# Pairing the odd token tiles of an attention + FFN kernel, with gate sums in other places, two single units and reordered last stores

## The chip, the cores and the metric

The kernel runs on one core of one Trainium2 chip. The metric is the device time of one execution in microseconds. Before the change the median of three runs is 400.83 us (400.82 to 401.29). The profile is one further execution; its run took 400.93 us, its span is 399.2 us.

## What is computed

```python
# q, k, v: (8 batches, 12 heads, 448 tokens, 64)
scores = (1 / sqrt(64)) * q @ k.T - log(448)
attn   = sigmoid(scores)
x      = (attn @ v)            # heads side by side: (3584 tokens, 768)
gate   = maximum(x @ w_gate, 0)        # (768, 1536)
val    = x @ w_val                     # (768, 1536)
out    = (gate * val) @ w_out          # (1536, 768), float32
```

The matmuls run in fp16 with fp32 sums.

## The kernel before

**Layout.** A batch has 448 tokens; two batches make a group of 896 tokens, four groups in all. The hidden activations of a group lie in hT: 12 units of 128 hidden features (on the partitions) by 896 tokens. 896 tokens are seven token tiles of 128; the seventh, tile 6, is the odd one.

**Attention.** A score unit (qk_unit, line 292) is one of 21 per batch: three groups of four heads by seven key chunks. It makes 4 matmuls into two PSUM banks, and ScalarE puts a sigmoid over each bank (line 187). After seven units of a head group, the PV matmuls (line 250) read the probabilities, and VectorE evicts two banks to xT (line 184).

**FFN in batches 0 and 1.** The ordinary form (gv, line 304): six matmuls for the gate, six for the value, a relu, and a multiply into hT (line 327).

**FFN in groups 1 to 3.** A fast 2x2 block product with seven block products in place of eight (Strassen-Winograd), in two places. In gv_pair (line 498) the blocks are halves of the 768 features, gate against value, and one batch of the group against the other; one item takes two units of 128 hidden features at once and holds six PSUM banks: b, c and a, each for two units. In down_pair (line 423) the blocks are two token tiles, halves of the hidden features, and halves of the output; it holds three banks b, c and a. In both the bank b is filled, copied out, and then accumulated on again; so is c. The order of products and copies in gv_pair is:

```python
product(b, 0, B11);  copy(0, b, first_copy)   # first_copy: VectorE, in the tail ScalarE
product(c, 3, T1);   copy(2, c)               # ScalarE
product(b, 4, T2, False);  copy(1, b)         # ScalarE
beside()                                      # next item's sums, then the slot's jobs
product(a, 1, B21);  plus(0, a)               # VectorE
product(b, 5, T3, False);  plus(2, b)
product(c, 6, B22, False); plus(1, c)
product(b, 2, T4, False)                      # then the gating: even batch, odd batch
```

The sums of blocks are made on VectorE: token_sums (line 406, four of 128x768), unit_sums (473, three of 128x768), batch_sums (492, over xT), weight_sums (395, over w_out, 128x2304), and gate_sums (469), which overwrite half of w_val once the ordinary form no longer needs it.

**Odd tiles.** Three pairs take tiles 0 to 5 of a group. Tile 6 goes through down (line 341): 12 matmuls of 512 columns and 12 of 256.

**Order of the work.** The order on every engine is the order of the program text; nothing reorders it. From batch 2 on, a batch is cut into slots: some score units (with the PV matmuls of a head group after the second unit in slots 0, 2 and 4), then one item from a hand-written queue named work (push_group, line 653; next_work, line 667). "Slot 4.1" below is slot 1 of batch 4. The items are w (a gate/value pair of units), y0 to y2 (a pair of token tiles) and t (the odd tile). prepare (line 659) makes the sums of the item that comes next. jobs are copies and DMA transposes for the next batch, loads, and batch sums; they stand inside the item, after its first copy (y) or after its third product (w). PSUM banks come from a ring of eight; later() chooses which banks are taken again last.

Of the kernel before, what the change touches and what calls it, by code (L numbers as in the profile page):

```python
# [17 lines left out]
def kernel(  # L18
# [244 lines left out]
    class FirstSlot:  # L263
# [6 lines left out]
        def unit(self, u):  # L270
            qn = self.qn
            cs = range(2 * u, min(2 * u + 2, NCH))
            ps = pairp.tile([P, 2, 512], FP32, tag="pair", name="qk_ps")
            for j, c in enumerate(cs):
                qk(
                    qkT_tiles[(0, self.g)], c, self.c0, self.c1,
                    lambda hh: ps[:, hh, j * qn : (j + 1) * qn],
                )
            i = (self.number * 4 + u) % 12
            PT = early.tile([P, 2, 512], FP16, tag=f"PT{i}", name="PT")  # L280
            n = qn * len(cs)
            sigmoid(PT[:, :, 0:n], ps[:, :, 0:n])
            for j in range(len(cs)):
                self.pieces.append(PT[:, :, j * qn : (j + 1) * qn])

# [17 lines left out]

    def gv(b, q0, qn, f, act_relu):
        ps = []
        for nm, wt in (("g_ps", wg), ("v_ps", wv)):
            ps.append(bank(nm))
            for dc in range(NDC):
                nc.tensor.matmul(  # L309
                    ps[-1][:, 0:qn],  # L310
                    wt[:, dc, f * P : (f + 1) * P],
                    xT_tiles[b][:, dc, q0 : q0 + qn],
                    start=(dc == 0),
                    stop=(dc == NDC - 1),
                )
        gate_sb = gsbp.tile([P, S], FP32, tag="gsb", name="gate_sb")
        if act_relu:
            nc.scalar.activation(gate_sb[:, 0:qn], ps[0][:, 0:qn], AF.Relu)  # L318
        else:
            nc.vector.tensor_scalar(  # L320
                out=gate_sb[:, 0:qn], in0=ps[0][:, 0:qn], scalar1=0.0, scalar2=None, op0=AOP.max
            )
        g = b // 2
        if g not in hT_tiles:
            hT_tiles[g] = hTp.tile([P, NFC, 2 * S], FP16, tag="hT", name="hT")
        o = (b % 2) * S + q0
        nc.vector.tensor_tensor(  # L327
            out=hT_tiles[g][:, f, o : o + qn],
            in0=gate_sb[:, 0:qn],
            in1=ps[1][:, 0:qn],  # L330
            op=AOP.mult,
        )
# [8 lines left out]
    def down(g, t):  # L341
        ysb = ysbp.tile([P, DM], FP32, tag="ysb", name="ysb")
        for nm, m0, m1 in (("ya", 0, 512), ("yb", 512, DM)):
            ps = bank(nm)
            for f in range(NFC):
                nc.tensor.matmul(  # L346
                    ps[:, 0 : m1 - m0],
                    hT_tiles[g][:, f, t * P : (t + 1) * P],
                    wo[:, f, m0:m1],
                    start=(f == 0),  # L350
                    stop=(f == NFC - 1),
                )
            nc.vector.tensor_scalar(
                out=ysb[:, m0:m1], in0=ps[:, 0 : m1 - m0], scalar1=OUT_SCALE, scalar2=None, op0=AOP.mult
            )
        store(g, t, ysb, 0, DM, (nc.sync, nc.sync))

# [7 lines left out]
    late = {}  # L365
    sums = {}

    def open_late():
        first_sbuf.close()
        pool = ctx.enter_context(tc.tile_pool(name="late", bufs=1))  # L370
        late["T"] = pool.tile([P, 4, HF, HM], FP16, tag="T", name="T")
        late["X"] = pool.tile([P, 3, HD, S], FP16, tag="X", name="X")
        late["sums"] = ctx.enter_context(tc.tile_pool(name="sums", bufs=2))
# [20 lines left out]

    def weight_sums(i):
        T = [late["T"][:, j] for j in range(4)]
        B11, B21 = wo[:, 0:HF, 0:HM], wo[:, HF:NFC, 0:HM]
        B12, B22 = wo[:, 0:HF, HM:DM], wo[:, HF:NFC, HM:DM]
        sub(T[i], *((B12, B11), (B22, T[0]), (B22, B12), (B21, T[1]))[i])

    def token_blocks(g, p):
        h = hT_tiles[g]
        t1, t2 = (slice(t * P, (t + 1) * P) for t in (2 * p, 2 * p + 1))
        return h[:, 0:HF, t1], h[:, HF:NFC, t1], h[:, 0:HF, t2], h[:, HF:NFC, t2]
# [18 lines left out]
    def down_pair(g, p, beside, then, last, first_copy):  # L423
        A11, A12, S3, A22 = token_blocks(g, p)
        S1, S2, S4 = sums.pop(("y", g, p))
        T1, T2, T3, T4 = (late["T"][:, i] for i in range(4))
        B11, B21, B22 = wo[:, 0:HF, 0:HM], wo[:, HF:NFC, 0:HM], wo[:, HF:NFC, HM:DM]
# [23 lines left out]
        plus(y2[:, hi], b)  # L451
        product(c, S4, B22, False)
        plus(y1[:, hi], c)
        if last:
            store(g, 2 * p, y1, 0, DM, (nc.sync, nc.scalar))
        else:
            store(g, 2 * p, y1, 0, DM, (nc.sync, nc.sync))
# [3 lines left out]
        if last:  # L461
            store(g, 2 * p + 1, y2, HM, DM, (nc.sync, nc.sync))
            store(g, 2 * p + 1, y2, 0, HM, (nc.sync, nc.scalar))
        else:
            store(g, 2 * p + 1, y2, 0, DM, (nc.sync, nc.sync))
# [7 lines left out]
    def unit_sums(g, f):  # L473
        S1, S2, S4 = sums_tile(2 * P)
        fs = slice(f * P, (f + 2) * P)
        A11, A12 = wg[:, 0:HD, fs], wg[:, HD:NDC, fs]
        S3, A22 = wv[:, 0:HD, fs], wv[:, HD:NDC, fs]
        sub(S2, A22, S3)
        nc.vector.tensor_tensor(out=S1, in0=S2, in1=A11, op=AOP.add)
        sub(S4, A12, S2)  # L480
        sums[("w", g, f)] = S1, S2, S4
# [10 lines left out]
    def batch_sums(g, ks):  # L492
        T1, T2, T4, _, B21, B12, B22 = batch_blocks(g, ks)
        sub(B12, B22, B12)
        sub(T2, B22, T1)
        sub(T4, B21, T2)

    def gv_pair(g, f, beside, first_copy):
# [3 lines left out]
        b, c, a = ([bank(nm) for _ in range(2)] for nm in ("u", "g2", "g1"))  # L502
        later((6, 7, 4, 5, 2, 3))
        gs = [[gsbp.tile([P, S], FP32, tag="gsb", name="gsb") for _ in range(3)] for _ in range(2)]
        if g not in hT_tiles:
            hT_tiles[g] = hTp.tile([P, NFC, 2 * S], FP16, tag="hT", name="hT")
        h = hT_tiles[g]
        sets = []
        for u in range(2):
            us, fs = slice(u * P, (u + 1) * P), slice((f + u) * P, (f + u + 1) * P)  # L510
            S1, S2, S4 = (t[:, :, us] for t in sums[("w", g, f)])
            sets.append((
                wg[:, 0:HD, fs], wg[:, HD:NDC, fs], wv[:, HD:NDC, fs],
                S1, S2, wv[:, 0:HD, fs], S4,
            ))
        del sums[("w", g, f)]

        def product(ps, i, W, first=True):
            for u in range(2):
                products([(ps[u], S, HD, sets[u][i], W, first)])  # L520

        def copy(i, ps, by=nc.scalar.copy):
            for u in range(2):
                by(gs[u][i][:], ps[u][:, 0:S])  # L524

        def plus(i, ps):
            for u in range(2):
# [3 lines left out]

        def gated(u, o, gate_sb, val):
            nc.vector.scalar_tensor_tensor(
                out=h[:, f + u, o : o + S], in0=gate_sb, scalar=0.0, in1=val, op0=AOP.max, op1=AOP.mult
            )
# [15 lines left out]
        for u in range(2):  # L551
            gated(u, 0, gs[u][0][:], b[u][:, 0:S])
        for u in range(2):
            gated(u, S, gs[u][1][:], gs[u][2][:])
# [97 lines left out]

    def push_group(g):
        tail = [("t", g, 6)] + [("y", g, p) for p in range(3)]
        if g == 0:
            tail.insert(0, tail.pop(1))
        work.extend([("w", g, f) for f in range(0, NFC, 2) if g > 0] + tail)
# [9 lines left out]
    def next_work(jobs=(), alone=False):  # L667
        kind, g, i = work.popleft()

        def beside():  # L670
            for job in jobs:
                job()

        if kind == "y":
            down_pair(g, i, beside, prepare, not work, scaled_act if alone else scaled)
        elif kind == "w":
            gv_pair(g, i, lambda: (prepare(), beside()), nc.scalar.copy if alone else nc.vector.tensor_copy)
        else:
            beside()
            prepare()  # L680
            down(g, i)

    ffn_mix(1, [(1, lambda: both(1, 0))])
    for b in range(1, B):
# [16 lines left out]
        elif b == 2:  # L701
            mix = (2, 2, 1, 1, 1, 2)
            hooks = {
                2: [(0, prepare)],
                4: [(1, lambda: weight_sums(0)), (0, lambda: weight_sums(1))],
# [3 lines left out]
        elif b == 3:  # L709
            mix = (1, 1, 1, 0, 0)  # L710
        else:
            mix = (0,) * count
        for m in range(count):
            jobs = []
            for i, (g, c) in enumerate(order[cuts[m] : cuts[m + 1]]):
                if m in pv_at and i == pv_at[m][1]:
                    if m == 0:
# [3 lines left out]
                        elif b % 2 == 0:  # L721
                            push_group(b // 2 - 1)
# [5 lines left out]
            if b == 2 and m == count - 1:  # L728
                jobs.append(lambda: (dma_transposes(3, 0), dma_transposes(3, 1)))
            elif b == 3 and m == count - 1:  # L730
# [12 lines left out]
            if b % 2 and b > 2:  # L743
                if m == count - 1:
                    jobs.append(lambda: (batch_sums_t1(b // 2), batch_sums(b // 2, (0, 1))))
            elif b > 3 and m == 0:
                jobs.append(lambda: batch_sums(b // 2 - 1, (1, HD)))
            if b == 2 and m == count - 1:
                ffn_mix(mix[m], hooks[m])
                next_work(jobs)  # L750
# [6 lines left out]
            if b == 3 and m == 3:  # L757
                for f in range(0, NFC, 2):
                    gate_sums(f, f + 2)
    pv_finish(B - 1)  # L760
    push_group(B // 2 - 1)
    next_work([lambda: batch_sums(B // 2 - 1, (1, HD))])
# [32 lines left out]
```

## Time and profile before

| | |
|---|---|
| runs | 400.82, 400.83, 401.29 us |
| span of the profile | 399.2 us, granted clock 0.999 |
| busy | PE 388.9, DVE 279.9, ACT 223.0, POOL 49.4 us |
| chain that ended last | PE 73%, DMA 14%, issue 6% |
| matmul groups L385 (block products) | from 93.5 us to the end |
| last matmul ends, last copy ends | 393.8, 394.65 us |

PE is TensorE's matmuls, PEld its weight loads, DVE VectorE, ACT ScalarE, POOL GpSimd, SP the queue that issues stores and transposes. In a timeline a line gives start and length in us, engine, line of the code, operation, what is written and read, how many instructions were merged, and in brackets how long the engine was idle before and what released it. In the list of waits the numbers are the total in us, how often, and the longest.

The items stand thus in the slots:

| where | before | after |
|---|---|---|
| 2.5, 3.3, 3.4 | y0, t, y1 | y0, y1, y2 |
| 4.0 to 4.4 | y2, w, w, w, w | w, w, w, w, w |
| 5.0 to 5.4 | w, w, t, y0, y1 | w, y3, y0, y1, y2 |
| 6.0 to 6.4 | y2, w, w, w, w | w, w, w, w, w |
| 7.0 to 7.4 | w, w, t, y0, y1 | single, single, y0, y1, y2 |
| after the last batch | y2, six w, t, y0, y1, y2 | six w, y3, y0, y1, y2 |

### The profile page before, as it was taken

The numbers are of one execution on the slowest core, as the hardware profiler recorded it, in microseconds if no ns is written. First come the engines' busy times: TensorE is split into PE (matmuls) and PEld (weight loads), VectorE is DVE, ScalarE is ACT, GpSimd is POOL, SyncE is SP. The second block draws the span as 40 slices with busy tenths as digits, with TensorE's granted clock in tenths as the row PEclk, the third lists the DMA queues.
The fourth block names the chain that finished last, engine by engine and source line by source line (L and its number), as shares of the span: only waits on it lengthen the run. The fifth ranks groups of instructions, "written<-read, shape, count | busy, mean of one in ns | idle before, by whom it ended". The sixth has DMA issues, their size and how long they took to land.

```text
span 399.2 us, 8737 instructions
## 1 busy us (share of the span) xinstructions
PE 388.9 (97%) x3488; PEld 217.9 (55%) x3488; DVE 279.9 (70%) x539; ACT 223.0 (56%) x475; POOL 49.4 (12%) x73
## 2 busy tenths in 40 slices
PE   8999999999998999999999999999999999999994
PEld 3678786545455554554555555455455555555562
DVE  2454344367358889999758889999766779887661
ACT  5946778783885565655665455565566234533131
POOL 8643301600030300003000300000000000000000
PEclk9999999999999999999999999999999999999999
DMA  9999994999897894224945695223012320000144
GB/s 149 199 199 204 205 141 94 177 203 187 178 161 152 165 204 76 46 48 51 178 85 133 130 218 89 48 24 61 12 40 80 80 79 2 0 2 0 39 115 124
DMA packets 68793, 43.69 MB, mean 109 GB/s; under 512 B 35856, under 2 KB 65296, under 8 KB 68752
## 3 DMA queue, kind: packets, MB, share of 16 engines
q0 software_dynamic: 30736, 23.33, 39.1%
q1 hardware_dynamic: 37584, 19.24, 23.0%
q8 instruction: 27, 0.44, 0.5%
q10 hardware_dynamic: 432, 0.56, 0.4%
q14 instruction: 14, 0.11, 0.1%
HBM read 47.19 MB, written 11.01 MB: 146 GB/s over the span
## 4 chain that ended last, share of the span: by engine, by line
PE 73%; DMA 14%; issue 6%; POOL 3%; DVE 2%; ACT 1%; ACTq 0%; POOLq 0%; DVEq 0%
PE u L385 32%; PE g L385 15%; PE y L385 9%; DMA v<-in_v_dram 6%; PE qk_ps L232 5%; PE pv_ps L250 5%; DMA wo<-in_moe_w_out_dram 4%; DMA k<-in_k_dram 4%; PE ya L346 3%; PE v_ps L309 1%; PE yb L346 1%; PE g_ps L309 1%; POOL q L110 1%; POOL k L110 1%; DVE wv L376 1%
## 5 line engine op out<-in xcount | busy, mean ns | idle before, releaser
L187 ACT ACTIVATE PT<-qk_ps 128x448 f16<-128x448 f32 (+3 forms) x318 | 150.6, 594 | 71.2 <-PE qk_ps L232 71.1
L385 PEld LDWEIGHTS <-S 128*128 128x128 f16 x540 | 52.8, 98 | 44.4 <-issue 0.8
L528 DVE TENSOR_TENSOR gsb<-g,gsb 128x448 f32<-128x448 f32 x72 | 43.0, 625 | 14.5 <-PE g L385 13.8
L232 PE MATMUL qk_ps<-qkT 64*64 64x448 f16 (+2 forms) x756 | 50.0, 336 | 0.9 <-DVE qkT L206 0.5
L421 ACT ACTIVATE ysb<-u 128x384 f32<-128x384 f32 x27 | 13.4, 498 | 56.3 <-PE u L385 56.3
L327 DVE TENSOR_TENSOR hT<-gate_sb,v_ps 128x256 f16<-128x256 f32 (+2 forms) x36 | 16.2, 465 | 33.5 <-ACT gate_sb L318 22.4
L385 PEld LDWEIGHTS <-hT 128*128 128x128 f16 x288 | 27.7, 98 | 21.0 <-issue 3.2
L524 ACT COPY gsb<-u 128x448 f32<-128x448 f32 x48 | 25.8, 566 | 23.9 <-PE u L385 22.9
L250 PE MATMUL pv_ps<-PT,v 64*64 64x448 f16 (+2 forms) x756 | 37.4, 329 | 0.4 <-issue 0.4
L184 DVE TENSOR_SCALAR xT<-pv_ps 128x448 f16<-128x448 f32 (+2 forms) x53 | 27.9, 567 | 13.4 <-PE pv_ps L250 12.1
L232 PEld LDWEIGHTS <-qkT 64*64 64x64 f16 x756 | 20.3, 105 | 24.9 <-issue 16.3
L309 PE MATMUL v_ps<-xT,wv 128*128 128x256 f16 (+2 forms) x216 | 33.3, 291 | 0.4 <-DVE hT L327 0.2
L309 PE MATMUL g_ps<-xT,wg 128*128 128x256 f16 (+2 forms) x216 | 33.5, 292 | 0.1
L385 PEld LDWEIGHTS <-wv 128*128 128x128 f16 x216 | 21.1, 98 | 19.8
L385 PEld LDWEIGHTS <-wg 128*128 128x128 f16 x216 | 20.3, 98 | 20.6 <-issue 3.0
L250 PEld LDWEIGHTS <-v 64*64 64x64 f16 x756 | 21.8, 107 | 11.8 <-issue 1.4
L385 PE MATMUL u<-T,hT 128*128 128x384 f16 x144 | 27.3, 326 | 0.0
L437 DVE SCALAR_TENSOR_TENSOR ysb<-y,ysb 128x384 f32<-128x384 f32 x24 | 13.4, 557 | 18.8 <-PE y L385 11.3
L110 POOL DMA_DIRECT2D k<-in_k_dram x14 | 10.9, 779 | 112.3 <-DVE rel L215 105.8
L309 PEld LDWEIGHTS <-wg 128*128 128x128 f16 x216 | 18.5, 98 | 11.5 <-issue 5.0
L309 PEld LDWEIGHTS <-wv 128*128 128x128 f16 x216 | 20.1, 98 | 8.2 <-DMA wv<-in_moe_w_val_dram 0.5
L385 PE MATMUL u<-xT,wg 128*128 128x448 f16 x108 | 23.5, 353 | 0.1
(67 smaller groups left out, 531.3 us busy)
## 6 DMA issues: line engine op xcount, KB each, us to landing
out_dram<-ysb SPq DMA_DIRECT2D x53, 192.0 KB, 2.9
k<-in_k_dram POOLq DMA_DIRECT2D x5, 672.0 KB, 11.8
q<-in_q_dram POOLq DMA_DIRECT2D x5, 672.0 KB, 14.9
v<-in_v_dram POOLq DMA_DIRECT2D x8, 336.0 KB, 15.6
v<-in_v_dram POOLq DMA_DIRECT2D x16, 168.0 KB, 15.3
k<-in_k_dram POOLq DMA_DIRECT2D x8, 224.0 KB, 10.4
wo<-in_moe_w_out_dram POOLq DMA_DIRECT2D x1, 1536.0 KB, 13.2
q<-in_q_dram POOLq DMA_DIRECT2D x6, 224.0 KB, 11.3
```

The lines of the kernel that those rows point to most:

```text
L110: nc.gpsimd.dma_start(t16[:, xs, cs], rows_of(src, b)[:, xs, cs])
L184: nc.vector.tensor_scalar(out=xT, in0=src, scalar1=XSCALE, scalar2=None, op0=AOP.mult)
L187: nc.scalar.activation(PT_ap, ps_ap, AF.Sigmoid, bias=sig_bias, scale=qk_scale)
L232: nc.tensor.matmul(out_of(hh)[o : o + 64, :], qkT[rows, c, cols], qkT[rows, NCH + c0 : NCH + c1, cols], start=True, stop=True, tile_positi ...
L250: nc.tensor.matmul(ps[hh][64 * r : 64 * r + 64, 0:qn], v16[rows, 2 * g + hh, c * D : (c + 1) * D], pieces[c][rows, hh, :], start=(c == 0), ...
L309: nc.tensor.matmul(ps[-1][:, 0:qn], wt[:, dc, f * P : (f + 1) * P], xT_tiles[b][:, dc, q0 : q0 + qn], start=(dc == 0), stop=(dc == NDC - 1),)
L327: nc.vector.tensor_tensor(out=hT_tiles[g][:, f, o : o + qn], in0=gate_sb[:, 0:qn], in1=ps[1][:, 0:qn], op=AOP.mult,)
L346: nc.tensor.matmul(ps[:, 0 : m1 - m0], hT_tiles[g][:, f, t * P : (t + 1) * P], wo[:, f, m0:m1], start=(f == 0), stop=(f == NFC - 1),)
L385: nc.tensor.matmul(ps[:, 0:n], A[:, k_, :], W[:, k_, :], start=(first and k_ == 0), stop=(k_ == kn - 1), skip_group_check=True,)
L421: nc.scalar.activation(o, ps[:, 0:HM], AF.Copy, scale=OUT_SCALE)
L524: by(gs[u][i][:], ps[u][:, 0:S])
L528: nc.vector.tensor_tensor(out=gs[u][i][:], in0=ps[u][:, 0:S], in1=gs[u][i][:], op=AOP.add)
```

## The change

- The odd tile of an even group is set aside in a buffer of its own, and multiplied together with the odd tile of the next group as a fourth token pair, y3. down is gone. The gating into hT is one fused max-and-multiply everywhere; for the odd batch of an even group it is cut at token 768, in two instructions.
- To make room, the difference of the w_out halves is written over w_out itself, and the probabilities of batch 0 lie in fitted buffers (first three slots) and in the later batches' pool.
- gate_sums, six in a row after slot 3.3 before, stand two by two: after 2.3, 3.0, 3.1 and inside 3.3.
- The queue moves up by one slot (table above), so that a w follows the PV matmuls in slots 4.0, 6.0 and after the last batch. There the second part of batch_sums is issued ahead of the item, and not as one of its jobs; within it T2 comes before B12.
- The last pair of units of group 2 is taken as two single units. The last w of a group no longer makes the next item's sums inside, but after its gating: after both batches' (group 1), after the even one (group 2), after the odd one (group 3). In group 2 the odd gating moves into the next item.
- The last item stores the right half of its second tile before the first tile, not after it.

```diff
@@ gating
+    def gated(g, f, o, n, gate_sb, val, relu=AOP.max):
...
+        end = o + n
+        cut = max(o, min(end, ASIDE)) if g % 2 == 0 else end
+        for a, z, dst in ((o, cut, hT_tiles[g]), (cut, end, late.get("aside"))):
+            if a < z:
+                d = 0 if dst is hT_tiles[g] else ASIDE
+                nc.vector.scalar_tensor_tensor(
+                    out=dst[:, f, a - d : z - d],
...
@@ token_blocks
+        if p == 3:
+            return late["aside"][:, 0:HF], late["aside"][:, HF:NFC], h[:, 0:HF, t1], h[:, HF:NFC, t1]
@@ down_pair
+        if last:
+            store(*to2, y2, HM, DM, (nc.sync, nc.sync))
         product(c, S4, B22, False)
         plus(y1[:, hi], c)
-        if last:
-            store(g, 2 * p, y1, 0, DM, (nc.sync, nc.scalar))
...
+        store(*to1, y1, 0, DM, (nc.sync, nc.scalar if last else nc.sync))
@@ batch_sums
+        sub(T2, B22, T1)
         sub(B12, B22, B12)
-        sub(T2, B22, T1)
@@ gv_units (was gv_pair)
+        if final == "even":
+            finish((True,))
+            prepare()
+            return lambda: finish((False,))
+        if final == "alone":
+            finish((False,))
+            prepare()
+            finish((True,))
+        else:
+            finish((True, False))
+            if final == "odd":
+                prepare()
@@ push_group
-        tail = [("t", g, 6)] + [("y", g, p) for p in range(3)]
...
+            pairs = [(f, f + 1) for f in range(0, NFC, 2)]
+            if g == B // 2 - 2:
+                pairs[-1:] = [(NFC - 2,), (NFC - 1,)]
+            work.extend([("w", g, fs) for fs in pairs])
+        work.extend([("y", g, p) for p in ((3, 0, 1, 2) if g % 2 else (0, 1, 2))])
@@ the loop over batches
+                3: [(0, lambda: (gate_sums(0, 2), gate_sums(2, 4)))],
...
+                0: [(0, lambda: gate_sums(4, 6))],
+                1: [(0, lambda: gate_sums(6, 8))],
+                2: [(0, prepare)],
...
+            elif b == 3 and m == count - 2:
+                jobs.append(lambda: (gate_sums(8, 10), gate_sums(10, 12)))
...
             elif b > 3 and m == 0:
-                jobs.append(lambda: batch_sums(b // 2 - 1, (1, HD)))
+                batch_sums(b // 2 - 1, (1, HD))
...
-            if b == 3 and m == 3:
-                for f in range(0, NFC, 2):
-                    gate_sums(f, f + 2)
     pv_finish(B - 1)
-    push_group(B // 2 - 1)
-    next_work([lambda: batch_sums(B // 2 - 1, (1, HD))])
+    batch_sums(B // 2 - 1, (1, HD))
     while work:
         next_work((), True)
```

## Prediction

> **What bounds the kernel now.** I read the page's busy lines first, then the list of waits for the matmul engine alone, then its timeline.
>
> ```profile
> PE 388.9 (97%) x3488; PEld 217.9 (55%) x3488; DVE 279.9 (70%) x539; ACT 223.0 (56%) x475; POOL 49.4 (12%) x73
> PE   8999999999998999999999999999999999999994
> DVE  2454344367358889999758889999766779887661
> PE u L385 <- DVE xT L184: 1.2, 1, 1.2
> PE u L385 <- DVE ysb L416: 0.6, 1, 0.6
> ```
>
> PE is busy in all slices but the first and last, and two waits for VectorE are the only ones over 0.2 us after the first pairs of down-projection start (93.5 us). TensorE is the bound: a matmul saved is time saved, and any new PE wait is time lost. DVE at 8 or 9 tenths has little room in places. The chain of waits says the same (PE 73%); its DMA share lies in the first 88 us, where PE is also full.
>
> ```profile
> 369.30 2.75 PE L346 MATMUL ya<-wo,hT 128*128 128x512 f16 x12
> 371.89 1.47 PE L346 MATMUL yb<-wo,hT 128*128 128x256 f16 x12
> 373.20 1.14 PE L385 MATMUL u<-wo,hT 128*128 128x384 f16 x6
> 380.03 1.14 PE L385 MATMUL u<-wo,hT 128*128 128x384 f16 x6
> ```
>
> Read start to start: an odd tile costs 373.20 - 369.30 = 3.90 us, a pair 380.03 - 373.20 = 6.83, so 0.975 per product. The same view of a slot with one gate/value pair, all engines:
>
> ```profile
> 279.95 1.14 DVE L533 SCALAR_TENSOR_TENSOR hT<-gsb,u 128x448 f16<-128x448 f32 x2
> 280.36 1.16 PE L232 MATMUL qk_ps<-qkT 64*64 64x448 f16 x16
> 280.85 3.60 ACT L187 ACTIVATE PT<-qk_ps 128x448 f16<-128x448 f32 x8 [4.39 <-PE qk_ps L232]
> 281.01 1.15 DVE L533 SCALAR_TENSOR_TENSOR hT<-gsb 128x448 f16<-128x448 f32 x2
> 281.15 0.10 PEld L232 LDWEIGHTS <-qkT 64*64 64x64 f16 x2 [0.27 <-issue]
> 281.46 1.31 PE L385 MATMUL u<-xT,wg 128*128 128x448 f16 x6
> 282.24 1.19 DVE L524 COPY gsb<-u 128x448 f32<-128x448 f32 x2
> 284.25 1.06 ACT L524 COPY gsb<-g 128x448 f32<-128x448 f32 x2
> 286.01 1.30 PE L385 MATMUL u<-xT,wv 128*128 128x448 f16 x6
> ```
>
> A product of two units takes 1.14 us, of one 0.57. A reader starts 0.21 after the matmuls it needs (281.46 + 0.57, copy at 282.24); PE resumes 0.05 after its release (DVE ends at 281.09, the weight load of the fourth score unit restarts at 281.15: that unit writes the banks that the even gating frees). ScalarE reaches its copies only behind eight sigmoids, 3.89 after the slot begins.
>
> [...] PE waited 0.57 us at 96.17 for a copy queued behind a weight sum. [...]
>
> **The gains.**
> - Pairing: four odd tiles go, 4 x 3.90 = 15.6; two pairs come, 2 x 6.83 = 13.66. PE gains 1.94.
> - Gate sums spread: six in a row (2.89 us) delayed the eviction of xT, and so the pair at 123.14 by 1.16. They now stand two by two in gaps of DVE (idle 1.75 before the weight sums at 88.14) or behind the first copy. Gain 1.16.
> - Stores at the end: four SP issues ran from 393.56 to 396.26, about 0.6 each, two of them data ready at 392.55. Put first, they leave SP free when the last copy ends (394.65), so its last issue starts about 394.7 instead of 395.7; ACT's issue at 394.68 is then as late. Between 0.3 and 1.0, taken 0.6.
>
> ```profile
> 393.56 2.70 SPq L339 DMA_DIRECT2D out_dram<-ysb  x4
> 394.16 0.49 ACT L421 ACTIVATE ysb<-u 128x384 f32<-128x384 f32 x1 [3.69 <-PE u L385]
> ```
>
> Together 3.70. First-slot probability tiles in other pools only remove waits; PE is full there, so nothing. Gating by one fused instruction has the price of the old multiply. No store or transpose passes another in a way that PE sees: loads of the next batch start some 4 us later in slots 4.0 and 6.0, and are needed three slots (28 us) on.
>
> **The new waits.** Each is a place where DVE or ACT, in order, hands PE a bank or a sum late (P is the end of the PV matmuls, E of the item before). I lay the two queues side by side with the steps that DVE's timeline shows in a stream (start to start): 0.53 to 0.57 for 448 columns out of PSUM, 0.59 for a token or unit sum that reads the one before it, 0.47 for one that doesn't, and for the sums over 128x896:
>
> ```profile
> 316.46 0.61 DVE L376 TENSOR_TENSOR xT<-xT 128x896 f16<-128x896 f16 x1
> 316.99 1.28 DVE L376 TENSOR_TENSOR X<-xT,X 128x896 f16<-128x896 f16 x2
> ```
>
> 1. *w0 in slots 4.0 and 6.0.* w0's third product may start only when the first product's bank is copied, by DVE, but the rest of the batch sums now stands ahead of that copy. DVE: two evictions from P+0.21 (1.07 and a drain) to P+1.35, three sums at about 0.53 to P+2.94, first copy done P+3.56. PE wants it at P+0.48+1.14+1.14 = 2.76, gets it at 3.62: 0.86. The lag stays: unit sums (1.52), rel copies, six plus steps; the last product waits 0.06, and the second even gating ends about 1.6 after PE's end, where 0.8 was usual, so the next slot's fourth score unit waits 0.75 for its bank. 1.67 each, 3.34. Before, a down-projection pair stood here and hid these sums.
> 2. *Tile pair of 1 in slot 5.1.* Token sums need both gatings of the last w. Gating ends E+1.87 after PE's end E (190.51 against 188.63); S1 is done at 2.42, and S2, S4, S3 and then the first copy follow on DVE, done at 4.56. PE wants S1 at E+2.16 (0.31 late) and then the first copy, 3.45, has it at 4.62: 1.17. Together 1.48. The odd tile that stood here needed no sums.
> 3. *Single units, 7.0 and 7.1.* Between two uses of bank b lies only one product, 0.57, and a copy needs 0.21+0.62+0.05. 7.1, from the slot's start: first product ends 1.67, DVE copy done 2.50, PE wants 2.24, starts 2.55 (0.31). Fifth product wants 3.69; ACT ends its sigmoids at 3.89, copies g to 4.31 and u to 4.84: starts 4.90 (1.21). Last product waits for the plus: 0.30. Sum 1.82. 7.0 has its PV between the sigmoids: 0.33+0.22+0.32 = 0.87.
> 4. *First pair after them, 7.2.* Even gating, token sums and evictions run into each other, first copy done 0.4 late: 0.38.
> 5. *Slot 3.3.* The pair follows the last ordinary unit at once; its four sums end at 117.1, the first copy at 117.66, PE wants 117.16: 0.56.
> 6. *Slot 2.5.* The gating of an odd batch is split into 320 and 128 columns[...]. It lengthens the wait at 96.17 by 0.1 and one at 90.08 by 0.1: 0.20.
> 7. *Tail, w5 to tile pair of 3.* Odd gating from 368.96 on DVE, S1 done 370.63, PE wants 370.28: 0.40.
>
> In the tail the first w now follows PV: its T2 is ready near P+1.4 and PE wants it at P+2.27, with ACT copying, so no wait.
>
> Sum 3.34 + 1.48 + 2.69 + 0.38 + 0.56 + 0.20 + 0.40 = 9.05. Net +5.35 us on the profiled span of 399.2 us (its run took 400.93, others 400.82 to 401.29): 400.83 + 5.35 = **406.2**. Each delay could be 0 where DVE's order leaves more room than I count, or a third larger where one lag runs into the next slot: the new waits lie between 5 and 11.5, the forecast's own range is 402.1 to 408.6.
>
> **Rivals.**
> - *Faster: the matmul stream alone decides.* If PE does not in fact stop for the first copies and sums, the 3.70 stand: 397.1. For it: PE shows almost no wait before, with the same copies in the same ring. Against it: 96.17 and 123.14, where it did stop, and the 0.57 between uses of b. It decides from new waits under 3.70 us: slots 7.0 and 7.1 alone have 2.69 by my count.
> - *Only the single units wait*, because the DVE backlogs are absorbed: 397.1 + 2.7 = 399.8. For it, DVE has idle gaps of 2.21 in slots without jobs; against, the gaps lie behind the late copies, not ahead.
> - *The backlogs add up*: a lag in 4.0, 5.1 or 6.0 hits each of the next two slots by another 0.5: 409.
> - *Half of the DVE waits hidden*: 3.2 less, 403.0; hidden further, 401.5.
>
> **Numbers.** Forecast 0.74, adding up 0.08, half hidden or more 0.06, single units only 0.05, matmul stream alone 0.07. A measurement here tells some 0.2% (0.8 us) from no change: faster 0.12, same 0.03, slower 0.85. The range, 401.8 to 408.6, holds the forecast's own and the half-hidden case down to its slower half; the two faster cases, 401.5 and the longest backlogs are left out, about 0.2 together.
>
> **What would show it.** In the profile after: PE waits for DVE gsb (first copy) near 0.9 in two slots, for ACT gsb near 1.2 in one; first products 1.1 apart replaced by gaps in two slots with x3 products; no 1.16 wait in batch 3; ya and yb gone; PE idle up by about 8 us though its matmul time falls by 2. Wrong if PE idle grows by under 3.7.

## The result, and the profile after

The changed kernel takes 406.62 us (median of 4 runs, 405.94 to 406.75). The kernel before, measured beside it on the same chip, takes 401.06 us (median of 4, 400.82 to 401.48). The ratio after to before is 1.0134, interval 1.0116 to 1.0152: the kernel became slower by 1.3%. The profiled span went from 399.2 to 404.7 us.

The page of the kernel after, first the busy time of each engine, then PE and DVE in 40 slices of the span, then the shares of the chain that ended last:

```profile
PE 390.0 (96%) x3476; PEld 217.0 (54%) x3476; DVE 284.3 (70%) x573; ACT 226.3 (56%) x482; POOL 49.5 (12%) x73
...
PE   8999999999999999999899999999899999999995
DVE  2454344377368899998756799998765798897561
...
PE 63%; DMA 14%; DVE 10%; issue 7%; POOL 3%; ACT 2%; ACTq 0%; DVEq 0%; POOLq 0%
```

The busy line misleads here. Twelve fewer matmuls are run, and by the start-to-start rates of the kernel before the two pairs take 1.94 us less than the four odd tiles; yet PE's busy time rises by 1.1 us. A likely reason, not tested: the ends of matmuls are modelled, and a group that is followed by a wait is drawn some 0.16 us into it (slot 4.0 below). The slices of PE hardly change: two eights inside the row, where before there was one. What tells is the last line: PE's share of the chain fell from 73% to 63%, and DVE has 10% where it had 2%. The list of waits of PE says where; the numbers are the total in us, how often, and the longest:

```profile
PE u L384 <- DVE ysb L418: 2.0, 4, 1.0
PE u L384 <- DVE gsb L522: 1.7, 3, 0.8
...
PE u L384 <- ACT gsb L522: 1.2, 1, 1.2
PE pv_ps L250 <- issue: 0.8, 1, 0.8
PE y L384 <- DVE S L411: 0.5, 2, 0.3
...
PE u L384 <- DVE gsb L526: 0.4, 2, 0.2
```

L418 and L522 are the first copies out of bank b in a pair of token tiles and in a pair of units; L411 is the first token sum, L526 the plus steps. Before, no such copy or sum was waited for over 0.2 us after the first pairs of token tiles had begun, apart from one copy (0.6). The 1.2 us wait for the eviction of xT in batch 3 is gone.

**Slot 4.0**, PE and DVE in the order of time (start, length, engine, line, what is written and read, and in brackets the engine's idle time before it and what ended that):

```profile
136.09 0.62 DVE L375 TENSOR_TENSOR X<-xT,X 128x896 f16<-128x896 f16 x1
136.32 1.30 PE L384 MATMUL g<-X,S 128*128 128x448 f16 x6
136.63 0.62 DVE L375 TENSOR_TENSOR xT<-xT 128x896 f16<-128x896 f16 x1
137.16 0.61 DVE L375 TENSOR_TENSOR X<-xT,X 128x896 f16<-128x896 f16 x1
137.70 1.14 DVE L522 COPY gsb<-u 128x448 f32<-128x448 f32 x2
138.37 1.30 PE L384 MATMUL u<-X,S 128*128 128x448 f16 x6 [0.75 <-DVE gsb L522]
```

The three batch sums stand on VectorE ahead of the copy of `u`. The second product starts at 136.32 and would be followed 1.14 us later, at 137.46; the third starts at 138.37, 0.05 after the first unit's bank has been copied (137.70 + 0.62). The delay is 0.91. The bracket shows only 0.75, since the modelled end of the group before (136.32 + 1.30 = 137.62) lies 0.16 past the start-to-start time: a delay is better read from starts.

**Slot 5.1**, where the pair of odd tiles now follows the last pair of units of its group:

```profile
195.13 1.15 PE L384 MATMUL u<-wo,aside 128*128 128x384 f16 x6
...
196.49 1.15 PE L384 MATMUL y<-T,S 128*128 128x384 f16 x6 [0.21 <-DVE S L411]
...
198.00 0.55 DVE L418 TENSOR_SCALAR ysb<-u 128x384 f32<-128x384 f32 x1
198.61 1.14 PE L384 MATMUL u<-T,S 128*128 128x384 f16 x6 [0.97 <-DVE ysb L418]
```

Undisturbed, products of a pair start 0.975 to 0.99 apart. Here they start 1.36 and 2.12 apart: first the sum S is late (0.37), then the copy, which DVE reaches only behind the sums (1.13). That is 1.5 us in all.

**Slot 7.1**, with a single unit:

```profile
288.85 3.60 ACT L187 ACTIVATE PT<-qk_ps 128x448 f16<-128x448 f32 x8 [2.71 <-PE qk_ps L232]
...
292.26 0.61 ACT L522 COPY gsb<-g 128x448 f32<-128x448 f32 x1
292.67 0.64 ACT L522 COPY gsb<-u 128x448 f32<-128x448 f32 x1
293.36 0.73 PE L384 MATMUL u<-xT,wv 128*128 128x448 f16 x3 [1.15 <-ACT gsb L522]
```

ScalarE works through eight sigmoids before it reaches the copies of `g` and `u`. The product that accumulates on `u` again cannot start before 293.36. With a pair of units twice as many matmuls lie ahead of this point, and the copies are ready in time: in slot 6.3, also behind eight sigmoids, the copies of `u` begin at 266.01, and the fifth product starts at 266.92, 1.13 after the fourth. The products of a single unit are no slower by themselves: three matmuls take 0.57 us from start to start (283.38 to 283.95 in slot 7.0), half of a pair's 1.14.

### The profile page after: what moved, and what is told of

Its sections match the earlier page's. It is cut to its first block, busy times and chain, and to the rows that moved or that the text cites. A ratio compares the mean times of both kernels' runs of the same rounds, so it can differ in the third digit from the quotient of the medians.

```text
span 404.7 us, 8751 instructions
## 1 busy us (share of the span) xinstructions
PE 390.0 (96%) x3476; PEld 217.0 (54%) x3476; DVE 284.3 (70%) x573; ACT 226.3 (56%) x482; POOL 49.5 (12%) x73
## 4 chain that ended last, share of the span: by engine, by line
PE 63%; DMA 14%; DVE 10%; issue 7%; POOL 3%; ACT 2%; ACTq 0%; DVEq 0%; POOLq 0%
PE u L384 29%; PE g L384 12%; PE y L384 9%; DMA v<-in_v_dram 6%; PE pv_ps L250 5%; PE qk_ps L232 4%; DMA wo<-in_moe_w_out_dram 4%; DMA wv<-in_moe_w_val_dram 4%; DVE gsb L526 2%; DVE hT L319 2%; PE v_ps L333 1%; PE g_ps L333 1%; DVE S L375 1%; DVE xT L184 1%; ACT PT L187 1%
## 5 line engine op out<-in xcount | busy, mean ns | idle before, releaser
L384 PEld LDWEIGHTS <-S 128*128 128x128 f16 x576 | 56.1, 98 | 52.0 <-issue 5.7
L526 DVE TENSOR_TENSOR gsb<-g,gsb 128x448 f32<-128x448 f32 x72 | 42.8, 623 | 12.5 <-PE g L384 12.2
L423 ACT ACTIVATE ysb<-u 128x384 f32<-128x384 f32 x32 | 15.9, 497 | 61.0 <-PE u L384 60.6
L384 PEld LDWEIGHTS <-hT 128*128 128x128 f16 x312 | 30.0, 98 | 21.2 <-issue 1.9
L522 ACT COPY gsb<-u 128x448 f32<-128x448 f32 x48 | 25.8, 556 | 25.8 <-PE u L384 24.8
L319 DVE SCALAR_TENSOR_TENSOR hT<-gate_sb,v_ps 128x256 f16<-128x256 f32 (+2 forms) x36 | 14.6, 420 | 32.1 <-ACT gate_sb L342 21.4
L440 DVE SCALAR_TENSOR_TENSOR ysb<-y,ysb 128x384 f32<-128x384 f32 x28 | 15.6, 557 | 26.2 <-PE y L384 19.1
L384 PEld LDWEIGHTS <-wv 128*128 128x128 f16 x216 | 21.1, 98 | 22.0 <-issue 2.7
L384 PE MATMUL u<-wo,hT 128*128 128x384 f16 x156 | 29.7, 326 | 0.1
L384 PE MATMUL u<-X,S 128*128 128x448 f16 x108 | 23.5, 352 | 1.8 <-DVE gsb L522 1.7
L384 PE MATMUL u<-xT,wv 128*128 128x448 f16 x108 | 23.5, 352 | 1.2 <-ACT gsb L522 1.2
```

The costliest lines, as they stand in the source:

```text
L319: nc.vector.scalar_tensor_tensor(out=dst[:, f, a - d : z - d], in0=gate_sb[:, a - o : z - o], scalar=0.0, in1=val[:, a - o : z - o], op0=relu,
L384: nc.tensor.matmul(ps[:, 0:n], A[:, k_, :], W[:, k_, :], start=(first and k_ == 0), stop=(k_ == kn - 1), skip_group_check=True,)
L423: nc.scalar.activation(o, ps[:, 0:HM], AF.Copy, scale=OUT_SCALE)
L440: nc.vector.scalar_tensor_tensor(out=o, in0=ps[:, 0:HM], scalar=OUT_SCALE, in1=o, op0=AOP.mult, op1=AOP.add)
L526: nc.vector.tensor_tensor(out=gs[u][i][:], in0=ps[u][:, 0:S], in1=gs[u][i][:], op=AOP.add)
```

## The experiments

Times are medians, compared with 406.62 us for the kernel after; a ratio is always to the kernel before, whose median beside the experiments was 401.03 to 401.22 us. In the code, `...` stands for lines left out. "Third product" and the like count in the order of gv_pair.

**ScalarE takes the first copy of w0 in slots 4.0 and 6.0.** This asks whether the order of DVE's queue, and not the batch sums or the PSUM banks as such, makes the wait.

```diff
-            first_copy = nc.scalar.copy if alone else nc.vector.tensor_copy
+            first_copy = nc.scalar.copy if alone or i == (0, 1) else nc.vector.tensor_copy
```

> The first copy of the first gate/value item in slots 4.0 and 6.0 is made by ScalarE in place of VectorE. In-order theory: VectorE's copy stands behind three batch sums, and ScalarE is free of sigmoids 2.2 us after the PV matmuls, so its copy ends at P+2.73 against P+2.76 wanted: both waits of 0.9 at the third product vanish, VectorE is two copies (1.07 us) less behind, and the waits of the next slots' score units (0.35 each) shrink. Some 1.8 to 2.5 us less than after: 404.1 to 404.8. Rival, that the wait is for the sum T2 and not for the copy: no change, 406.6.

Measured 404.47 us (404.06 to 404.86), ratio 1.0084 [1.0069, 1.0099]. Slot 4.0 in its timeline:

```profile
136.17 1.30 PE L384 MATMUL g<-X,S 128*128 128x448 f16 x6
136.72 1.05 ACT L522 COPY gsb<-u 128x448 f32<-128x448 f32 x2
...
137.38 1.29 PE L384 MATMUL u<-X,S 128*128 128x448 f16 x6
```

The products now start 1.21 apart, 0.07 more than undisturbed. The sums are still made, on the same engine at the same point of the slot; only the copy no longer stands behind them. One line of code gives back 2.15 us, so the queue was the cause. With the smaller lag, the later delay at the fourth score unit, in slots 4.1 and 6.1, shrinks from 0.35 to 0.13 each; with the 0.85 at each third product that makes 2.1 us.

**The pair of odd tiles last in its group** (group 1 only, so in slot 5.4; the even gating then precedes the sums of y0).

```diff
-        work.extend([("y", g, p) for p in ((3, 0, 1, 2) if g % 2 else (0, 1, 2))])
+        work.extend([("y", g, p) for p in {1: (0, 1, 2, 3), 3: (3, 0, 1, 2)}.get(g, (0, 1, 2))])
...
-                rest = gv_units(g, i, beside, first_copy, "alone" if alone else ("even", "odd")[g % 2])
+                rest = gv_units(g, i, beside, first_copy, "alone" if alone else "even")
```

> In group 1 the pair of odd tiles comes last of the four token pairs, and only the even gating of the last gate/value item stands ahead of the sums for the next pair, the odd gating moves into the next item. In-order theory: the sums start 1.05 us earlier, so the wait for S1 (0.37) goes and the wait for the first copy falls from 1.13 to some 0.4: about 1.1 us less, 405.5. Rival, that the waits come from the pair of odd tiles itself (its buffer, its place on PE): they follow it to slot 5.4, and the time stays at 406.6.

Measured 405.15 us (405.06 to 405.46), ratio 1.0103 [1.0088, 1.0118]: 1.47 us less. The two waits of slot 5.1 (0.37 and 1.13) become one of 0.44, and slot 5.4 has none, which is 1.06; the other 0.4 lies within what the kernels differ by in the first 95 us, where this edit changes nothing (see below). The wait belonged to a pair that needs *both* gatings at once, as the prediction had it. A pair of even tiles can start behind one.

**VectorE makes the copies of the fourth step of single units,** in place of ScalarE.

```diff
-        copy(1, b)
+        copy(1, b, nc.vector.tensor_copy if len(fs) == 1 else nc.scalar.copy)
```

> In the two single units the copy after the third product is made by VectorE in place of ScalarE. In-order theory: in slot 7.1 ScalarE reached it only behind eight sigmoids and another copy; on VectorE it ends some 0.85 after the third product, and PE's wait of 1.3 before the fifth product falls to 0.3. Slot 7.0 stays within 0.2. About 0.9 us less: 405.7. Rival, that the wait is for something else that ScalarE or its sigmoids hold (a bank, the c copy): 406.6.

Measured 406.5 us (406.41 to 406.95), ratio 1.0138 [1.0121, 1.0155]: no gain. In slot 7.1 the edit did what was expected of it: the wait before the fifth product fell from 1.31 to 0.31. But in slot 7.0 the timeline has

```profile
287.69 0.61 DVE L526 TENSOR_TENSOR gsb<-u,gsb 128x448 f32<-128x448 f32 x1
288.36 0.73 PE L384 MATMUL u<-X,wv 128*128 128x448 f16 x3 [1.30 <-DVE gsb L526]
```

The plus step on `u` must be done before its last product, and it now stands on DVE behind the added copy, the next unit's sums and the relative-position copies: 1.46 late where it was 0.38. I had placed the copy in slot 7.1's queue and not counted what it pushes back in 7.0. The time agrees with the rival's number, but not with its reason: a wait was removed and another took its place.

**No single units.** The last two units stay a pair, so that slot 7.4 has no item, only its jobs.

```diff
-            if g == B // 2 - 2:
-                pairs[-1:] = [(NFC - 2,), (NFC - 1,)]
...
+            elif b == B - 1 and m == count - 1:
+                prepare()
+                for job in jobs:
+                    job()
```

> The last two units of group 2 are taken as one pair, so the queue of items is empty in slot 7.4, which then has score units, PV and sums only. If the single units' waits (0.9 + 2.0 us) are their own, they go, and the empty slot costs what ScalarE needs for ten sigmoids (4.3 us) beyond the 2.6 us of matmuls there, part of it hidden in the tail: between 1 us less and 1 us more than after, 405.6 to 407.6. If splitting costs nothing and the waits only stand in for ScalarE's work, the empty slot adds its 1.7 us on top: over 408.

Measured 404.8 us (404.13 to 405.36), ratio 1.0092 [1.0075, 1.011]: 1.8 us less, where the expectation ran from one less to one more. The waits of the single units were 0.92 in 7.0 and 2.00 in 7.1, 2.92 in all, and they are gone. The price is the hole in slot 7.4, whose PV matmuls have nothing beside them:

```profile
319.46 2.25 PE L250 MATMUL pv_ps<-PT,v 64*64 64x448 f16 x26 [0.15 <-DVE xT L184]
```

They are drawn out at the pace of the sigmoids, ten of which run from 316.81 for 4.47 us (28 of these matmuls take 1.45 us when the probabilities are ready). From the first score unit of the slot to the first product after it 5.32 us pass (316.32 to 321.64). In the kernel after, the score units of this slot take 2.71 (313.04 to 315.75) and the PV matmuls 1.45 (322.67 to 324.12), together 4.16. The hole costs 1.16, and 2.92 - 1.16 = 1.76 agrees with the measured gain. Filling the hole cost more than the hole: I had priced the hole too high, and the time lies outside the expected range.

**The six gate sums in a row again,** behind slot 3.3. (In the kernel after they stand two behind 2.3, one behind 3.0, one behind 3.1 and two inside 3.3, not two by two throughout.)

```diff
-                3: [(0, lambda: (gate_sums(0, 2), gate_sums(2, 4)))],
...
-                0: [(0, lambda: gate_sums(4, 6))],
-                1: [(0, lambda: gate_sums(6, 8))],
...
-            elif b == 3 and m == count - 2:
-                jobs.append(lambda: (gate_sums(8, 10), gate_sums(10, 12)))
...
+            if b == 3 and m == 3:
+                for f in range(0, NFC, 2):
+                    gate_sums(f, f + 2)
```

> The six gate sums stand in a row after slot 3.3 again, all else as after. If spreading them was what removed the wait of 1.2 us in slot 3.4, it comes back: six steps of 0.48 us ahead of two evictions of xT, and the first product of the pair waits for its bank: 1.0 to 1.3 us more, 407.6 to 407.9. Rival, that the wait went because the odd tile no longer stands in slot 3.3: no change, 406.6.

Measured 409.84 us (409.3 to 411.34), ratio 1.0221 [1.0205, 1.0237]: 3.2 us more, against some 1.2 expected. The place was right and the size wrong. Lines of its timeline, DVE and PE in slot 3.4:

```profile
125.23 2.89 DVE L375 TENSOR_TENSOR wv<-wg,wv 128x768 f16<-128x768 f16 x6
128.04 1.15 DVE L184 TENSOR_SCALAR xT<-pv_ps 128x448 f16<-128x448 f32 x2
128.71 1.14 PE L384 MATMUL u<-wo,hT 128*128 128x384 f16 x6 [2.50 <-DVE xT L184]
```

In the new order the four token sums of y2 (2.1 us) stand ahead of the gate sums. So the evictions start at 128.04 and not at 125.26 as in the kernel after, and the pair that needs their banks waits. At this place it is 2.57 us, and the two spans differ by 2.6; in the new order, spreading the gate sums is worth about twice the 1.2 us that it was worth in the old one. (The medians differ by 3.2, but the runs of this kernel lie 2 us apart.)

**The last stores as before.** The store of the second tile's right half goes behind the last copies again.

```diff
-        if last:
-            store(*to2, y2, HM, DM, (nc.sync, nc.sync))
         product(c, S4, B22, False)
...
         if last:
+            store(*to2, y2, HM, DM, (nc.sync, nc.sync))
             store(*to2, y2, 0, HM, (nc.sync, nc.scalar))
```

> The last item stores the right half of its second tile after the first tile again. From the profiles the reordering gained 0.4 us between the end of the last matmul and the end of the span (5.3 before, 4.9 after), and that comes back: 0.4 us more, 407.0. Rival, that the landings and not the issues set the end: within 0.2 us of 406.6, with the last issue later and the last landing not.

Measured 406.65 us (405.99 to 407.36), ratio 1.0136 [1.0123, 1.0149]. The median shows no difference (0.03 us), so the time is inconclusive. In the profiles, from the end of the last matmul to the end of the span it is 5.30 us here, 4.93 in the kernel after and 5.31 before. So reordering the stores is worth 0.37 in the tail, less than what runs of one kernel differ by.

**Only the odd tiles of groups 2 and 3 are paired;** those of 0 and 1 go through down again, there are no single units, and the queue stands where it stood. (The third sum of the w_out blocks has a buffer of its own, so that down finds w_out whole, and the probability pool has ten buffers.)

```diff
...
+        work.extend({
+            0: [("y", g, 0), ("t", g, 6), ("y", g, 1), ("y", g, 2)],
+            1: [("t", g, 6)] + [("y", g, p) for p in range(3)],
+            2: [("y", g, p) for p in range(3)],
+            3: [("y", g, p) for p in (3, 0, 1, 2)],
+        }[g])
...
-                batch_sums(b // 2 - 1, (1, HD))
+                jobs.append(lambda: batch_sums(b // 2 - 1, (1, HD)))
```

> Only the odd tiles of groups 2 and 3 are paired; those of 0 and 1 go through the ordinary product as before, so the queue has an item for each slot with no single units, and slots 4.0, 6.0 and 5.1 have the items of before. Gate sums and last stores as after; the difference of the w_out halves has its own buffer, and the probabilities ten buffers in place of eleven. If the loss of after comes from the moved queue (w after PV, pair after w, single units) and not from the pairing itself: before less 0.97 (PE), 1.2 (slot 3.4), 0.4 (stores), plus 0.5 (tail) and 0.4 (slot 7.2): 399.3 to 400.0. If pairing itself costs (the buffer set aside, split gating), over 401.1.

Measured 400.1 us (399.16 to 400.93), ratio 0.9968 [0.9961, 0.9975]: faster than the kernel before, and just above the range expected. Of the large new waits only those at the first copy in 7.2 (0.39) and at the tail's first sum (0.50) remain; the one at the first copy in 2.5 (0.73) is as long as it was before. The count of items explains why the others are absent. There are 23 slots with an item (2.5, 3.3, 3.4, and five in each of batches 4 to 7). Groups 0 to 2 had 24 items for them, 4 + 10 + 10, and the last, y2 of group 2, was left over behind slot 7.4. One pairing uses up that spare item. A second one leaves a slot empty, which the change fills by splitting a pair; and the pairing of groups 0 and 1 moves all later items up by one slot, w0 to where the batch sums are made.

**The mirror: only groups 0 and 1 are paired,** no single units, everything from 3.3 on one slot early as in the kernel after.

```diff
...
+        work.extend({
+            0: [("y", g, p) for p in range(3)],
+            1: [("y", g, p) for p in (3, 0, 1, 2)],
+            2: [("t", g, 6)] + [("y", g, p) for p in range(3)],
+            3: [("t", g, 6)] + [("y", g, p) for p in range(3)],
+        }[g])
...
```

> The mirror case: only the odd tiles of groups 0 and 1 are paired, no single units, but the queue stands one slot earlier from slot 3.4 on, so w follows PV in 4.0 and 6.0 and the tile pair follows w in 5.1. If the loss comes from the moved queue and the single units: after plus 0.97 (PE), less 2.9 (units), 0.4 (slot 7.2), 0.5 (tail): 403.8, slower than before though the pairing is worth the same 0.97 as that of groups 2 and 3, which was faster. If the single units are all of the loss: 400 to 401.

Measured 403.38 us (403.3 to 404.24), ratio 1.0063 [1.005, 1.0076]: slower than before with one pairing and the same matmul gain. Its waits stand where the kernel after has them: 0.92 at w0 in each of 4.0 and 6.0 and 0.35 at the fourth score unit behind each, 0.37 and 1.13 in 5.1, 0.32 in 3.3. So it is not the pairing but the place to which it moves the items that costs time: the two mirror kernels differ by 3.3 us.

**One pairing (groups 2 and 3), and ScalarE for the first copy in slot 2.5.** This is one more edit to the kernel that pairs groups 2 and 3 alone:

```diff
-            down_pair(g, i, beside, then, not work, scaled_act if alone else scaled)
+            down_pair(g, i, beside, then, not work, scaled_act if alone or (g, i) == (0, 0) else scaled)
```

> As the kernel with only groups 2 and 3 paired, and the first copy of the first token pair (slot 2.5) on ScalarE, which is idle there, in place of VectorE behind a weight sum: the wait of 0.6 to 0.8 us at the third product goes, 0.6 us less than that kernel, 398.7 to 399.4. Rival: ScalarE's other copies come later by one, and the wait moves to the fifth product: no gain.

Measured 399.03 us (398.38 to 400.65), ratio 0.9952 [0.9937, 0.9966]. This beats both kernels, by 2.0 and 7.6 us. What remains of PE's waits beyond the start of the kernel is

```profile
PE pv_ps L250 <- issue: 0.5, 1, 0.5
PE y L401 <- DVE S L428: 0.3, 1, 0.3
PE u L401 <- DVE ysb L435: 0.2, 1, 0.2
```

that is, a gap near 23 us of which more is said below, the tail's first sum and the copy in 7.2 (L401, L428 and L435 are the lines 384, 411 and 418 of the kernel after).

This kernel is faster than the one before, but not by its pairing. All that the pairing of groups 2 and 3 changes in the order of the work lies between slot 4.0 and the end, and slot 4.0 has y2 in both kernels. The first product of that slot and the last of the kernel are, before and then here,

```profile
132.26 1.15 PE L385 MATMUL u<-wo,hT 128*128 128x384 f16 x6
392.70 1.14 PE L385 MATMUL u<-T,hT 128*128 128x384 f16 x6
```

```profile
130.20 1.15 PE L401 MATMUL u<-wo,hT 128*128 128x384 f16 x6
390.58 1.14 PE L401 MATMUL u<-T,hT 128*128 128x384 f16 x6
```

From start to start this is 260.44 and 260.38 us: the waits of 0.39 and 0.50 take back nearly all of the 0.97 that the pairing saves. The spans differ by 2.6 us. Of these 1.84 lie between the first block product and slot 4.0, where the gate sums are spread and the copy in 2.5 has moved, and 0.4 behind the last matmul, where the stores are reordered.

**Both pairings kept, all repairs at once:** ScalarE's first copy at w0 and in 2.5, y3 last in group 1, no single units.

> Both pairings are kept; put together are the ScalarE copy in slots 4.0 and 6.0 (2.1 us by its own run), the tile pair last in group 1 (1.1 by its waits), no single units (1.8) and the ScalarE copy in slot 2.5 (0.6). If the waits are separate places that do not hide one another, the gains add: 406.6 less 5.6, 401.0, at the time of before and slower than the kernel that pairs groups 2 and 3 alone (399.0). If they hide one another, 402.5 or more.

Measured 400.68 us (400.38 to 401.21), ratio 0.9991 [0.9983, 1.0]. The three gains found singly are 2.15, 1.47 and 1.82, together 5.44; the copy in 2.5 was worth 1.07 in the kernel with one pairing, which makes 6.51. The whole gain is 5.94. So the causes are separate, and add up to within 0.6 us. Even so repaired, two pairings are not better than one: 1.65 us slower. The hole in slot 7.4 (1.16) takes back a little more than the second pair saves (0.97), and delays remain in 3.3 (0.31), 5.1 (0.44) and around w0 in 4.0 and 6.0 (0.5 together).

## Why the prediction was right, step by step

The forecast, 406.2, lies within the runs of the kernel after, and its mechanism held: hand-overs by engines that work in order cost PE more (8.4 us of waits) than the matmuls saved (1.94). That it comes so near is in part luck, as shown below the table. Delays below are from start to start in the profile of after, against the same items before.

| step of the prediction | predicted | in the profile | tested by |
|---|---|---|---|
| 1. w0 in 4.0 and 6.0, first copy | 0.86 each | 0.91, 0.92 | first copy on ScalarE: 0.07 |
| 1. last product; fourth score unit after it | 0.06; 0.75 each | 0; 0.35 each | first copy on ScalarE: 0; 0.13 |
| 2. pair of 1 in 5.1 | 1.48 | 1.50 | y3 last: 0.44 |
| 3. single units, 7.0 and 7.1 | 0.87; 1.82 | 0.92; 2.00 | no single units: gone |
| 4. first pair after them | 0.38 | 0.38 | not singly |
| 5. slot 3.3 | 0.56 | 0.31 | not singly |
| 6. split gating, slots 2.4 and 2.5 | 0.20 | 0.29 | not singly |
| 7. tail, w5 to y3 | 0.40 | 0.50 | not singly |
| sum of the waits | 9.05 | 8.4 | |
| gate sums spread | 1.16 | about 1.2 | back in a row: +3.2 |
| stores | 0.6 | 0.4 | as before: inconclusive in time |

Four terms were mis-sized.

- *The fourth score unit, 0.75.* I let DVE's lag run on at 1.13 to 1.21 us for two plus steps, numbers from a slot in which DVE waits for PE, and slower than the 0.53 to 0.57 a step that the prediction itself names. With a backlog DVE goes faster: two plus steps take 1.06 (they start at 140.89, 141.96 and 143.02) against 1.14 for PE's product of two units, so it catches up by some 0.07 at each pair. In the timeline of after the gating and the score unit that waits for its banks are

```profile
144.08 1.14 DVE L319 SCALAR_TENSOR_TENSOR hT<-gsb,u 128x448 f16<-128x448 f32 x2
...
145.27 0.38 PE L232 MATMUL qk_ps<-qkT 64*64 64x448 f16 x3 [0.18 <-DVE hT L319]
```

The gating ends at 145.22, 1.18 after PE's end at 144.04, and not 1.6.

- *The stores, 0.6.* SP's last issue indeed starts earlier, 0.83 us after the last matmul's end where it was 1.88. But the span then ends 4.09 us after the start of that issue and not 3.43, so that 0.4 of the 1.05 us gained at the issue reaches the end. I had priced the issue alone and not the landing; why that is longer is not shown.
- *Slot 3.3, 0.56.* Measured 0.31; the sums and the first copy end some 0.2 sooner after the item's start than laid out.
- *Split gating, 0.20.* Measured 0.29, of which 0.24 is a wait in slot 2.4 that grew from 0.36 to 0.60. The 0.1 for each of two waits was my estimate, shown by no trace of before. In the profiles a gating in two parts takes 0.60 us to the start of the next instruction (90.09 to 90.69), a whole one 0.53 (89.42 to 89.95 before), so 0.07 of the 0.24 is the split. The weight sum that stands ahead of the gating starts when a load of w_out has landed: at 88.81 us here, 0.27 ahead of the gate product at 89.08, and at 88.14 before the change, 0.44 ahead of the one at 88.58. The other 0.17 is thus the load's. This number is not steady: in six experiments with the same code there the wait is 0.4 to 1.0, and the one that pairs groups 0 and 1 has none.

**What the sum did not have.** By places the net is 8.4 - 1.94 - 1.2 - 0.4 = 4.9 us, but the spans differ by 5.5. Most of the rest is one gap in the first 95 us, while inputs are still being loaded (the load of w_out in the chain of after lasts from 72.70 to 88.72). The kernel after has near 23 us

```profile
22.89 0.32 PE L250 MATMUL pv_ps<-PT,v 64*64 64x192 f16 x5 [0.83 <-issue]
```

and the kernel before has 0.37 at the same matmul. In the ten experiments this gap was between 0.3 and 1.1 us, though none of them edits the code of this matmul, and the first block product started between 93.3 and 94.3 (93.5 before, 94.2 after). So this part is no effect of the change that I can show; that the forecast is nearer to the runs than its sum of waits warrants (9.05 against 8.4) is partly due to it, which is luck.

Of the rivals, "the matmul stream alone" and "only the single units wait" are refuted by the waits in 4.0, 5.1 and 6.0, each removed by moving one copy or one item. "Half of the DVE waits hidden" is refuted by the same places. "The backlogs add up" was wrong in the other direction: the lag shrinks in the following slot.

**What stays open.** Why PE pauses at this one matmul near 23 us was not tried. The waits of steps 4, 5, 6 and 7 were read from the profile and not undone one at a time, except the copy of 2.5 within the kernel with one pairing. And no kernel was run that has the spread gate sums, the reordered stores and the copy of 2.5 on ScalarE but no pairing; by the stretches above it should be as fast as the best one here, 399.0 us, which is an estimate.

## What to carry to other kernels

In a kernel whose engines work in program order (in slot 4.0 DVE starts the copy of `u` at 137.70, behind three sums; in the first experiment ScalarE, without them ahead, at 136.72), count the items of a hand-written queue against its slots before removing one: a saved item moves all later ones, and each must still find its banks copied and its sums made where it lands. Lay the in-order queue of each helper engine beside the matmul stream, start to start, and look at what stands ahead of every copy that frees a bank; moving the first copy to the other engine in two slots gave 2.15 us here, while one pairing saves 0.97 us of matmuls. A saving belongs where the queue has an item to spare: there one pairing came out even, while both together made the kernel 1.3% slower. And when a variant is faster, compare it with the kernel before stretch by stretch: the best one here gains 2.0 us, and next to nothing of it in the stretch that the pairing changes.

## What the runs showed that I had not expected

- A hole of one item in the queue cost 1.16 us, time in which the PV matmuls trickle behind the sigmoids. The two single units that filled it, with only 0.57 us of other matmuls between two uses of a bank, cost 2.92.
- DVE with a backlog does two plus steps in 1.06 us, 6 to 12% less than the 1.13 to 1.21 where it waits for PE, so a lag shrinks from step to step.
- The last store was issued 1.05 us sooner after the last matmul, and the kernel ended only 0.4 sooner after it.
- PE pauses for 0.3 to 1.1 us at the same matmul near 23 us in all twelve kernels, and its length changes from kernel to kernel, also where their code there is the same.
